# Loading the first eight chunks of q and k in pairs, eight rows a partition

## The chip, the cores and the metric

The kernel runs on one core of one Trainium2 chip. The metric is the device time of one execution in microseconds (us); the figure for the kernel before is the median of three runs. Engines are named as the profile names them: PE does matrix multiplies (PEld its weight loads), DVE vector work, ACT activations, POOL and SP here mostly issue DMAs. A DMA that changes the type of the data (float32 in memory, float16 on the chip) is called a casting load here, one that keeps float32 a direct load.

## The reference

Four batches of a cross-covariance attention, followed by one feed-forward block over all 24320 rows. N is 6080, C is 256, Dff is 2048, all inputs are float32 and tau is 1.

```python
qn = q / (norm(q, axis=1) + 1e-6)          # norms over the N rows, per column
kn = k / (norm(k, axis=1) + 1e-6)
s = kn.T @ qn / tau                        # 256 x 256 per batch
a = softmax(s, axis=-1)
x = (v @ a).reshape(4 * 6080, 256)
r = maximum(x @ w_in, 0)                   # 256 -> 2048
out = (s_moe * r * r + b) @ w_out          # 2048 -> 256
```

## The kernel before

**What is computed where.** For each batch, a 256 x 256 product of q and k over all 6080 rows (matmuls of line 154 into `s_ps`), the squared column norms of q and k, and from both a softmax matrix that is folded into `w_in` (`wa`). After that the batch needs only v: groups of 512 rows are transposed (`vT`) and multiplied with `wa` (line 761), squared, and multiplied with `w_out` (line 932, 836 and 808). Batches 1 to 3 have their q and k work spread over the steps of the v groups before them; only batch 0 has nothing to hide behind. It is the stage from 0 to about 38 us, and this change is made in it.

**Batch 0.** Its rows are cut into 13 chunks (`chunks_first`): eleven of 512 rows, four rows to a partition, then one of 256 and one of 192 rows. `load(c)` takes a tile `qk` (q and k of the chunk, 4 KB a partition) from the pool `qk_pool` of eight buffers and issues one DMA for k and one for q. Three of the first four transfers are direct loads into the float32 tile `raw32`: k of chunk 0 in two halves of 64 partitions, on the SP and the ACT queue, q of chunk 0 on the ACT queue, k of chunk 1 on the SP queue. `cast` then turns them into float16: the k parts on DVE, the q part on ACT (both are line 145 in the profile). All others are casting loads on the POOL queue (line 137), in order of chunk, k ahead of q. The last three chunks come with all three k parts first and then the q parts. Behind them in the same queue are v of the first group (line 458), `w_in` in five pieces (line 522), v, and `w_out` in four float32 pieces `w32` (line 537), which take buffers from the same pool and tag as `qk`.

**What a chunk does to the engines.** Eight matmuls of line 154; a square of k on ACT (line 185) and of q on DVE for even chunks (line 182) or on ACT for odd ones; two fold additions (line 199) and one addition into the running sum (line 213), all on DVE. Chunks 5 to 9 also have one or two idle matmuls (line 554), which only keep PE busy. After chunk 9 the squares of the late chunks 10 to 12 go to PE directly (lines 229, 179, 252), and then come a chain of logarithms and exponentials on ACT (line 277), the softmax (line 308) and the first block of `wa` (lines 329 to 359). The first matmul of line 761 follows.

**What sets the order.** Every instruction is kept in program order on its engine (`po`), and so are the DMAs of one queue. A load waits until all readers of the buffer's last contents are done: with eight buffers, chunk 8 takes the buffer of chunk 0, the `w_out` pieces those of four chunks of the middle, and in batch 1 chunks 4 to 7 those of the `w_out` pieces. The pieces are read until the casts of line 638 (`T3`), steps 34 to 40 of the main loop. Loads of later batches are put 16 steps ahead of their first matmul, but POOL runs ahead of that: it follows its own order, not the steps.

Of the kernel before, what the change touches and what calls it, by code (L numbers as in the profile page):

```python
# [8 lines left out]
FP16 = mybir.dt.float16  # L9
FP32 = mybir.dt.float32  # L10
# [6 lines left out]
def kernel(  # L17
# [12 lines left out]
    nc = tc.nc  # L30
    P = 128

    B, N, C = q.shape
# [17 lines left out]
    NLATE = 3  # L51
# [3 lines left out]
    def po(ins):  # L55

        tc.keep_in_program_order(ins)
        return ins

    def pool(name, bufs, **kw):  # L60
        return ctx.enter_context(tc.tile_pool(name=name, bufs=bufs, **kw))
# [1 line left out]
    PSUM = bass.MemoryType.PSUM  # L63
    consts = pool("consts", 1)
    wpool = pool("wpool", 1)
    qk_pool = pool("qk_pool", 8)
    sq_pool = pool("sq_pool", 2)
    late_pool = pool("late_pool", 1)
    f3_pool = pool("f3_pool", 13)
# [5 lines left out]
    gpool = pool("gpool", 2)  # L75
# [17 lines left out]


    JC = 4
    DIRECT = ((0, 0), (0, 1), (1, 0))
    NDIRECT = 2

    def make_chunks(rows_of):
        chunks, at = [], 0  # L100
# [11 lines left out]
    class Gram:  # L112


        def __init__(self, b, chunks):
            self.b, self.chunks = b, chunks
            self.tiles = {}
            self.raw, self.rows, self.n_ps = {}, ([], []), [None, None]

        def load(self, c, parts=(0, 1)):  # L120

            at, np_, jc = self.chunks[c]
            if 0 in parts:
                self.raw[c] = qk_pool.tile([P, 2, JC, C], FP16, tag="qk", name="qk")
            t = self.raw[c]
            for i in parts:
                src = (k, q)[i]
                rows = src[self.b, at : at + np_ * jc, :].rearrange("(p j) c -> p j c", j=jc)
                if self.b == 0 and (c, i) in DIRECT:
                    if c == i == 0:  # L130
                        for h, queue in enumerate((nc.sync, nc.scalar)):
                            ps = ts(h, P // 2)
                            queue.dma_start(out=raw32[ps, 0], in_=rows[ps])
                    else:
                        (nc.sync, nc.scalar)[i].dma_start(out=raw32[:, DIRECT.index((c, i))], in_=rows)
                else:
                    po(nc.gpsimd.dma_start(out=t[:np_, i, :jc, :], in_=rows))
            self.tiles[c] = t[:, 1], t[:, 0]

        def cast(self, c):  # L140

            qc, kc = self.tiles[c]
            for i, (dst, copy) in enumerate(((kc, nc.vector.tensor_copy), (qc, nc.scalar.copy))):
                if (c, i) in DIRECT:
                    po(copy(out=dst, in_=raw32[:, DIRECT.index((c, i))]))  # L145

        def start(self):
            self.s_ps = ps_gram.tile([P, CH, C], FP32, tag="s_ps", name="s_ps")
# [306 lines left out]
    def load_v(g):  # L455
        t0, nj = group(g)
        v16 = vpool.tile([P, TG // P, C], FP16, tag="v16", name="v16")
        po(nc.gpsimd.dma_start(  # L458
            out=v16[:, :nj, :],
            in_=v_flat[t0 : t0 + nj * P, :].rearrange("(p j) c -> p j c", j=nj)))  # L460
        v_tiles[g] = v16
# [30 lines left out]
    nc.vector.memset(ones32, 1.0)  # L492
    grams = {b: Gram(b, chunks_first if b == 0 else chunks_later) for b in range(B)}
    g0 = grams[0]
    raw32 = gpool.tile([P, len(DIRECT), JC, C], FP32, tag="g16", name="raw32")

    po(nc.scalar.preload_act_table_set("natural_log_exp_and_others"))
    tiny = consts.tile([P, 1], FP32)
# [2 lines left out]
    nc.vector.memset(eps, EPS)  # L501
    ones_id = consts.tile([P, P], FP16)
    po(nc.vector.tensor_copy(out=ones_id, in_=fill.bitcast(FP32)[:, :P]))
    for c in range(NDIRECT):
        g0.load(c)
        g0.cast(c)
    for c in range(NDIRECT, len(g0.chunks) - NLATE):
        g0.load(c)
        if c == NDIRECT:
            po(nc.gpsimd.affine_select(  # L510
                out=ident16, in_=ones_id, compare_op=ALU.is_equal, fill=0.0, base=0,
                pattern=[[-1, P]], channel_multiplier=1))

    for parts in ((0,), (1,)):
        for c in range(len(g0.chunks) - NLATE, len(g0.chunks)):
# [14 lines left out]
    w_out_rows = moe_w_out.rearrange("(fo p) d -> p fo d", p=P)  # L530
# [2 lines left out]
    NPIECE = FT // 4  # L533
    w_pieces = []
    for i in range(NPIECE):
        w32 = qk_pool.tile([P, 4, C], FP32, tag="qk", name="w32")
        po(nc.gpsimd.dma_start(out=w32, in_=w_out_rows[:, ts(i, 4), :]))
        w_pieces.append(w32)
    load_v(2)
    s_bc = consts.tile([P, 1], FP32)  # L540
    po(nc.gpsimd.dma_start(out=s_bc, in_=moe_s.to_broadcast((P, 1))))
# [126 lines left out]
    for i, f in enumerate(folds):  # L668
        early.setdefault(FOLDS[i], []).append(f)
    at_step(14, lambda: po(nc.vector.tensor_scalar_mul(  # L670
        out=s_out, in0=s_bc, scalar1=1.0 / (LAM * LAM))))
# [29 lines left out]
    for b in range(1, B):  # L701
# [6 lines left out]
        n = NCH * JC  # L708
# [247 lines left out]
    for s in range(NS + FT):  # L956
# [9 lines left out]
        if work:  # L966
            items, n = work[0]
# [61 lines left out]
```

## Time and profile before

| | |
|---|---|
| median of three runs | 714.37 us (714.33 to 714.67) |
| span of the profiled execution, first to last instruction | 712.9 us |
| what lies around the span, against the median | 1.5 us |
| PE busy | 692.9 us (97%) |
| DVE, ACT, POOL busy | 635.6, 547.5, 114.1 us |
| first matmul of batch 0 (line 154) | starts at 10.96 us |
| first matmul of the main loop (line 761) | starts at 37.84 us |
| mean clock granted to PE | 0.998 |

The span is what the profile sees, so every sum is made in it, and a difference in it is carried to the median unchanged. The profile has no total for its own execution apart from the span; the median lies 1.5 us above it. Of the views, the chain of waits says what ended last in each stretch; the timeline lists the instructions with the idle time of their engine ahead of them and what ended it; the table of windows gives busy times and the rate of the DMAs. That rate counts bytes as written to the destination: a casting load that reads 4 KB counts 2 KB, a direct one counts all it reads.

### The profile page before, as it was taken

To read this page: it belongs to the slowest core of one execution; us is meant where nothing else is said; L and a number is where in the kernel's file an instruction comes from. 1 tells how busy PE (TensorE), PEld (TensorE's weight loads), DVE (VectorE), ACT (ScalarE), POOL (GpSimd) and SP (SyncE) were. 2 spreads that over 40 slices of the span, in tenths; PEclk is the share of its full clock that TensorE was granted. 3 is DMA by queue.
4 is the path that set the end of the run, shared out by engine and by line. 5 is a ranking of instruction groups with operands and counts; after the bars stand their busy time and mean duration, and the time that the engine had idled before them with its cause. 6 is when DMAs were issued, how large, how long until landed. Compare 5 with 4: busy or idle time off the path is not lost.

```text
span 712.9 us, 17531 instructions
## 1 busy us (share of the span) xinstructions
PE 692.9 (97%) x7422; PEld 502.9 (71%) x7422; DVE 635.6 (89%) x906; ACT 547.5 (77%) x598; POOL 114.1 (16%) x192
## 2 busy tenths in 40 slices
PE   3699999999999999999999999999999999999998
PEld 2456777776677777777677777777768777777777
DVE  4889999999988989998999899998998888888886
ACT  5689877787777777778877777777876777777875
POOL 4533132201202222111010222111000000000000
PEclk9999999999999999999999999999999999999999
DMA  9999999566566878465761888737323333321202
GB/s 213 207 259 168 186 164 137 114 109 122 105 136 109 133 137 144 110 92 101 156 131 50 148 134 150 129 76 96 101 65 75 94 71 75 97 61 46 83 31 75
DMA packets 87854, 83.55 MB, mean 117 GB/s; under 512 B 56368, under 2 KB 62784, under 8 KB 87776
## 3 DMA queue, kind: packets, MB, share of 16 engines
q0 software_dynamic: 27136, 44.00, 38.9%
q1 hardware_dynamic: 60128, 37.45, 21.1%
q8 instruction: 58, 0.95, 0.6%
q10 hardware_dynamic: 512, 0.98, 0.4%
q14 instruction: 20, 0.16, 0.1%
HBM read 78.91 MB, written 24.90 MB: 146 GB/s over the span
## 4 chain that ended last, share of the span: by engine, by line
PE 95%; DMA 4%; ACT 1%; issue 0%; DVE 0%; ACTq 0%; POOLq 0%
PE h_ps L761 46%; PE o_ps L932 40%; PE s_ps L154 5%; DMA qk<-in_q_dram 2%; DMA qk<-in_k_dram 1%; PE wa_ps L394 1%; PE o_ps L836 1%; PE o_ps L808 0%; PE wa_ps L336 0%; ACT r L277 0%; PE n_ps L252 0%; ACT sq L185 0%; ACT eT L308 0%; PE vT_ps L469 0%; DVE half L229 0%
## 5 line engine op out<-in xcount | busy, mean ns | idle before, releaser
L771 ACT ACTIVATE r<-h_ps 128x1024 f16<-128x1024 f32 (+1 forms) x384 | 388.5, 1013 | 144.2 <-PE h_ps L761 140.6
L761 PE MATMUL h_ps<-vT,wa 128*128 128x512 f16 (+7 forms) x1632 | 452.1, 364 | 0.5 <-ACT wa L329 0.5
L932 PEld LDWEIGHTS <-S 128*128 128x128 f16 x2944 | 198.1, 98 | 84.3
L932 PEld LDWEIGHTS <-g 128*128 128x128 f16 x2208 | 155.0, 98 | 74.0
L784 DVE TENSOR_TENSOR g<-r 128x2048 f16<-128x2048 f16 (+2 forms) x150 | 174.4, 1163 | 10.1 <-ACT r L771 9.7
L932 PE MATMUL o_ps<-T,S 128*128 128x128 f16 x2208 | 183.1, 219 | 0.0
L761 PEld LDWEIGHTS <-wa 128*128 128x128 f16 x1632 | 136.6, 98 | 19.0 <-ACT wa L329 1.0
L932 PE MATMUL o_ps<-w_out,g 128*128 128x128 f16 x1472 | 134.2, 219 | 0.0
L782 ACT ACTIVATE g<-r 128x1024 f16<-128x1024 f16 (+1 forms) x97 | 100.3, 1034 | 0.2
L789 DVE SCALAR_TENSOR_TENSOR o_sb<-o_ps,s_out,u 128x256 f32<-128x256 f32 x138 | 66.2, 480 | 36.1 <-PE o_ps L932 34.5
L154 PE MATMUL s_ps<-qk 128*128 128x256 f16 (+1 forms) x384 | 71.0, 287 | 15.6 <-ACT qk L145 11.0
L458 POOL DMA_DIRECT2D v<-in_v_dram x48 | 31.4, 662 | 239.9 <-DMA vT<-v 192.7
L215 POOL DMA_DIRECT2D f<-f x33 | 28.8, 874 | 245.9 <-DVE f L199 197.3
L789 DVE SCALAR_TENSOR_TENSOR u<-o_ps,s_out,rowconst 128x256 f32<-128x256 f32 x138 | 65.7, 476 | 0.0
L932 PE MATMUL o_ps<-w_out,S 128*128 128x128 f16 x736 | 63.5, 219 | 0.0
L932 PE MATMUL o_ps<-N,g 128*128 128x128 f16 x736 | 63.4, 219 | 0.0
L185 ACT ACTIVATE sq<-qk 128x1024 f16<-128x1024 f16 (+2 forms) x53 | 54.5, 1041 | 4.5 <-DMA qk<-in_k_dram 1.9
L861 DVE TENSOR_TENSOR S<-S,g 128x2048 f16<-128x2048 f16 (+1 forms) x47 | 56.4, 1200 | 1.2
L859 DVE TENSOR_TENSOR S<-g 128x2048 f16<-128x2048 f16 (+1 forms) x47 | 56.0, 1192 | 0.0
L863 DVE TENSOR_TENSOR S<-g 128x2048 f16<-128x2048 f16 x46 | 55.8, 1214 | 0.0
L865 DVE TENSOR_TENSOR S<-g,S 128x2048 f16<-128x2048 f16 x46 | 55.8, 1213 | 0.0
L154 PEld LDWEIGHTS <-qk 128*128 128x128 f16 (+1 forms) x384 | 33.0, 103 | 21.2 <-ACT qk L145 11.0
(103 smaller groups left out, 334.4 us busy)
## 6 DMA issues: line engine op xcount, KB each, us to landing
out_dram<-o_sb SPq DMA_DIRECT2D x43, 512.0 KB, 3.0
v<-in_v_dram POOLq DMA_DIRECT2D x47, 256.0 KB, 5.0
qk<-in_q_dram POOLq DMA_DIRECT2D x43, 256.0 KB, 7.7
qk<-in_k_dram POOLq DMA_DIRECT2D x42, 256.0 KB, 6.4
f<-f POOLq DMA_DIRECT2D x30, 128.0 KB, 3.1
vT<-v SPq DMA_TRANSPOSE x182, 3.0
w<-in_moe_w_out_dram POOLq DMA_DIRECT2D x4, 512.0 KB, 9.9
out_dram<-o_sb SPq DMA_DIRECT2D x8, 256.0 KB, 4.1
```

The costliest lines, as they stand in the source:

```text
L154: po(nc.tensor.matmul(self.s_ps[:, ch, :], qc[:np_, j, ts(ch, P)], kc[:np_, j, :], start=(c == 0 and j == 0 and ch == 0), stop=(c == len(s ...
L185: po(nc.scalar.activation(out=st["sq"][:np_, a, js, :], in_=(qc, kc)[a][:np_, js, :], func=AF.Square))
L761: po(nc.tensor.matmul(dst, wa[:, ci, ts(m, P)], src, start=(ci == 0), stop=(ci == CH - 1), skip_group_check=True))
L771: po(nc.scalar.activation(out=r16[:, :, i % 2, :n], in_=h_tiles.pop((g, i))[:, :, :n], func=AF.Relu))
L782: po(nc.scalar.activation(out=dst, in_=src, func=AF.Square))
L784: po(nc.vector.tensor_mul(dst, src, src))
L789: po(nc.vector.scalar_tensor_tensor(out=dst, in0=src, scalar=s_out, op0=ALU.mult, in1=add, op1=ALU.add))
L859: po(nc.vector.tensor_add(T[1], A21, A22))
L861: po(nc.vector.tensor_sub(T[2], T[1], A11))
L863: po(nc.vector.tensor_sub(T[3], A11, A21))
L865: po(nc.vector.tensor_sub(T[4], A12, T[2]))
L932: po(nc.tensor.matmul(st[name][:, j, :], a()[:, i, ts(j, P)], w[:, i, :], start=first, stop=last, skip_group_check=True))
```

## The change

The first eight chunks of batch 0 are loaded as four pairs. One DMA brings k of both chunks of a pair and one DMA q, 512 KB read becoming 1 MB, and each partition reads eight rows (8 KB) that lie in one piece, where it read four rows (4 KB). The tile of a pair holds both chunks, so the pool has four buffers of 8 KB for eight of 4 KB. Single loads (batch 0 from chunk 8 on, and all of batches 1 to 3) fill one half of such a tile. Direct loads are now only k of the first pair, as two halves of 64 partitions on the SP and ACT queues; q of the first pair goes to the POOL queue with a cast. Both casts of `raw32` are on DVE, and the q cast on ACT is gone. The `w_out` pieces take two tiles of two pieces each. The `affine_select` that makes the identity stands behind the second pair's loads.

```diff
-    qk_pool = pool("qk_pool", 8)
+    qk_pool = pool("qk_pool", 4)
...
-    DIRECT = ((0, 0), (0, 1), (1, 0))
-    NDIRECT = 2
+    NPAIRS = 4
...
+        def place(self, c):
+
+            if c // 2 not in self.raw:
+                self.raw[c // 2] = qk_pool.tile([P, 2, 2 * JC, C], FP16, tag="qk", name="qk")
+            t = self.raw[c // 2][:, :, (c % 2) * JC : (c % 2 + 1) * JC]
+            self.tiles[c] = t[:, 1], t[:, 0]
+            return t
+
         def load(self, c, parts=(0, 1)):
 
             at, np_, jc = self.chunks[c]
-            if 0 in parts:
-                self.raw[c] = qk_pool.tile([P, 2, JC, C], FP16, tag="qk", name="qk")
-            t = self.raw[c]
+            t = self.place(c)
             for i in parts:
                 src = (k, q)[i]
                 rows = src[self.b, at : at + np_ * jc, :].rearrange("(p j) c -> p j c", j=jc)
-                if self.b == 0 and (c, i) in DIRECT:
-                    if c == i == 0:
-                        for h, queue in enumerate((nc.sync, nc.scalar)):
-                            ps = ts(h, P // 2)
-                            queue.dma_start(out=raw32[ps, 0], in_=rows[ps])
-                    else:
-                        (nc.sync, nc.scalar)[i].dma_start(out=raw32[:, DIRECT.index((c, i))], in_=rows)
+                po(nc.gpsimd.dma_start(out=t[:np_, i, :jc, :], in_=rows))
+
+        def load_pair(self, n):
+
+            for c in (2 * n, 2 * n + 1):
+                self.place(c)
+            at = self.chunks[2 * n][0]
+            for i in range(2):
+                rows = (k, q)[i][self.b, at : at + P * 2 * JC, :].rearrange("(p j) c -> p j c", j=2 * JC)
+                if n == 0 and i == 0:
+                    for h, queue in enumerate((nc.sync, nc.scalar)):
+                        ps = ts(h, P // 2)
+                        queue.dma_start(out=raw32[ps], in_=rows[ps])
                 else:
-                    po(nc.gpsimd.dma_start(out=t[:np_, i, :jc, :], in_=rows))
-            self.tiles[c] = t[:, 1], t[:, 0]
+                    po(nc.gpsimd.dma_start(out=self.raw[n][:, i], in_=rows))
 
         def cast(self, c):
 
-            qc, kc = self.tiles[c]
-            for i, (dst, copy) in enumerate(((kc, nc.vector.tensor_copy), (qc, nc.scalar.copy))):
-                if (c, i) in DIRECT:
-                    po(copy(out=dst, in_=raw32[:, DIRECT.index((c, i))]))
+            po(nc.vector.tensor_copy(out=self.tiles[c][1], in_=raw32[:, ts(c, JC)]))
...
-    raw32 = gpool.tile([P, len(DIRECT), JC, C], FP32, tag="g16", name="raw32")
+    raw32 = gpool.tile([P, 2 * JC, C], FP32, tag="g16", name="raw32")
...
-    for c in range(NDIRECT):
-        g0.load(c)
-        g0.cast(c)
-    for c in range(NDIRECT, len(g0.chunks) - NLATE):
-        g0.load(c)
-        if c == NDIRECT:
+    for n in range(NPAIRS):
+        g0.load_pair(n)
+        if n == 0:
+            for c in range(2):
+                g0.cast(c)
+        if n == 1:
             po(nc.gpsimd.affine_select(
                 out=ident16, in_=ones_id, compare_op=ALU.is_equal, fill=0.0, base=0,
                 pattern=[[-1, P]], channel_multiplier=1))
+    for c in range(2 * NPAIRS, len(g0.chunks) - NLATE):
+        g0.load(c)
...
     for i in range(NPIECE):
-        w32 = qk_pool.tile([P, 4, C], FP32, tag="qk", name="w32")
-        po(nc.gpsimd.dma_start(out=w32, in_=w_out_rows[:, ts(i, 4), :]))
-        w_pieces.append(w32)
+        if i % 2 == 0:
+            w32 = qk_pool.tile([P, 8, C], FP32, tag="qk", name="w32")
+        w_pieces.append(w32[:, ts(i % 2, 4)])
+        po(nc.gpsimd.dma_start(out=w_pieces[i], in_=w_out_rows[:, ts(i, 4), :]))
```

## The prediction

> **What bounds the kernel now.** I read the chain of waits first. From 37.84 us on nearly every piece of it is PE, which is busy for all but about 3 of the last 675 us; the change takes no matmul away there, so all it can do is move the start of that stretch. Ahead of it the chain is this (start, length, what):
>
> ```profile
> 1.30 7.22 DMA qk<-in_q_dram
> 8.80 10.44 DMA qk<-in_q_dram
> 19.28 1.05 PE s_ps L154 x8
> 21.00 9.47 DMA qk<-in_k_dram
> 30.49 1.06 ACT sq L185
> 32.06 0.95 PE n_ps L252 x7
> 33.03 0.48 ACT r L277
> ```
>
> Up to 30.49 us the path is loads of q and k; after that it is a short chain over ACT, DVE and PE. The timeline shows how regularly chunks arrive: PE starts chunks 5 to 9 at 19.28, 21.74, 24.30, 26.76 and 29.31 us, the first four after idling for the q load.
>
> ```profile
> 19.28 1.05 PE L154 MATMUL s_ps<-qk 128*128 128x256 f16 x8 [0.95 <-DMA qk<-in_q_dram]
> ...
> 26.76 1.66 PE L154 MATMUL s_ps<-qk 128*128 128x256 f16 x8 [1.18 <-DMA qk<-in_q_dram]
> ...
> 30.37 0.69 DVE L199 TENSOR_TENSOR f<-sq 128x1024 f16<-128x1024 f16 x1 [1.08 <-ACT sq L185]
> ```
>
> That is (29.31 - 19.28) / 4 = 2.51 us a chunk of 1.049 MB read, 418 KB/us. Ten chunks at this pace would begin at 29.31 - 25.1 = 4.2 us. The third view is the table of windows; its last two columns are the DMA share and the GB/s written:
>
> ```profile
> 2.00:4.00 2.00, 0.00 (x0) 0.00 (x0) 0.00 (x0) 0.09 (x1) 1.94 (x5) 1.00 0.86 211
> 4.00:6.00 2.00, 0.00 (x0) 0.00 (x0) 0.24 (x1) 0.00 (x0) 2.00 (x4) 1.00 1.05 257
> 6.00:8.00 2.00, 0.00 (x0) 0.00 (x0) 0.56 (x1) 0.00 (x0) 0.04 (x1) 1.00 1.05 339
> 8.00:10.00 2.00, 0.00 (x0) 0.00 (x0) 0.69 (x1) 0.14 (x1) 0.73 (x1) 1.00 1.11 267
> ...
> 18.00:20.00 2.00, 1.05 (x11) 0.70 (x9) 1.83 (x5) 1.65 (x2) 1.01 (x2) 1.00 1.11 207
> ```
>
> The DMA engines never rest between 4 and 30 us: they are the bound. But the first 10 us move less. Up to 10 us, 2 x (211 + 257 + 339 + 267) = 2148 KB were written; the three direct loads are 1573 KB of it, so 575 KB came from casts, which read 1150 KB. Together 2.72 MB were read from about 2.75 us, when the windows of 0.25 us first show steady traffic, in 7.25 us. At 418 to 420 KB/us this takes 6.5: some 0.77 us are lost while direct loads run.
>
> **Part 1: fewer direct bytes.** Direct loads fall from 1573 to 1049 KB; q of the first pair becomes a casting load. If the 0.77 us go with the direct bytes, a third goes: -0.26 us. A second row gives the same size. POOL's waits on the transfer eight back show the landings (start, issue time, idle ahead of it in brackets):
>
> ```profile
> 40.37 0.55 POOL L541 DMA_DIRECT2D s_bc<-in_moe_s_dram  x1 [0.58 <-DMA w_in<-in_moe_w_in_dram]
> 41.60 0.54 POOL L543 DMA_DIRECT2D b_bc<-in_moe_b_dram  x1 [0.68 <-DMA w_in<-in_moe_w_in_dram]
> 42.88 0.53 POOL L458 DMA_DIRECT2D v<-in_v_dram  x1 [0.74 <-DMA v<-in_v_dram]
> 44.66 0.53 POOL L458 DMA_DIRECT2D v<-in_v_dram  x1 [1.24 <-PE wa_ps L336]
> 46.15 0.53 POOL L137 DMA_DIRECT2D qk<-in_k_dram  x1 [0.96 <-DMA w<-in_moe_w_out_dram]
> 47.41 0.53 POOL L137 DMA_DIRECT2D qk<-in_q_dram  x1 [0.73 <-DMA w<-in_moe_w_out_dram]
> ```
>
> Casting loads of 524 KB (w_in, then v) land 1.23 and 1.28 us apart. The four uncast w_out pieces of 524 KB land about 1.49 us apart on average: by my count of the queue they free the issues from 44.66 to 49.15 us, 4.49 us for three gaps. One 524 KB load turned from direct to casting is then worth 1.25 - 1.49 = -0.24 us. I take -0.25; ends: 0 (the start-up loss has nothing to do with casts) and -0.77.
>
> **Part 2: 8 KB rows in the stream.** Seven casting loads of 1.049 MB replace thirteen of 0.524 MB. The trace has no 8 KB row. The w_in loads of the rows above read 2 KB pieces, the v load 4 KB pieces, and both take about 1.25 us for 524 KB: the length of a piece does not show. I take 0. Lower end: charge the whole difference of the 1 KB w_out pieces to the number of pieces (32 an engine against 8, 0.24 us, 0.01 us a piece); 8 KB rows save four pieces an engine per 524 KB, and fourteen such halves give -0.56 us. Upper end: the worst pace that the trace has for these rows, the 2.72 / 7.25 = 0.375 MB/us of the first stage, for all 7.34 MB: 7.34 x (1/0.375 - 1/0.418) = +2.0 us.
>
> Fewer loads do not mean fewer fixed costs on the path: up to eight are in flight and they land 1.25 us apart, back to back. The Trainium skill's "DMA: Bandwidth & Descriptors", section "Measured", puts a load at 2.0 us plus its bytes at 436 KB a us and asks for 1 MiB each. My estimate by that formula, with loads taken one after another, is 13 x 3.2 - 7 x 4.4, some 11 us gained, and 703.6 us in all; the landings above, 1.23 to 1.28 us apart, contradict it for a filled queue. Against the change speaks the same page's "SWDGE vs HWDGE vs iDMA", where a packet is preferably at most 4096 B; the page gives no price for a longer one, and this trace shows none, so it adds nothing to the sum.
>
> **Part 3: arrival in pairs.** With the stream's origin at 4.2 - 0.25, pair n is complete at 3.95 + 5.02 (n + 1): 8.97, 13.99, 19.01, 24.03 us; chunk 8 at 26.5, chunk 9 at 29.06 (29.31 before). The first k casts are on DVE, 0.80 and 0.69 us in the trace; ACT loses its q cast of 1.04 us, and PE can start near 9.1 for 10.96. None of that counts, as PE waits for loads from 19.28 us anyway. What may count is the last pair. DVE's cadence is 2.3 us for an even chunk (26.89 to 28.86, and 0.34 to the next start) and 1.53 for an odd one (25.36 to 26.89). From 24.03: chunk 6 to 26.3, chunk 7 to 27.9, chunk 8 to 30.2. The fold of chunk 9 needs ACT's square of its q, 1.06 after 29.06, so 30.12: it starts at 30.2, against 30.37 before. Of 0.25 us gained, about 0.07 are lost here: **+0.07**. Ends: 0, and +0.7 if the pair's second chunk (1.53 us of DVE) waits half its length longer than I count. PE has 16 matmuls for the pair, 2.1 us at full clock (1.05 for eight), 3.3 at the granted clock of 0.50 between 27 and 30.4 us (1.66 for eight), and is free again for chunk 8 or within a microsecond of it.
>
> **Part 4: fewer buffers.** The load of chunk 8 waits for all readers of chunks 0 and 1. ACT's three squares (about 1.0 each) and PE's 16 slow matmuls end near 12.4 us, the load was issued at 15.99 before. By then 8 MB are issued and 3.4 have arrived: 11 us of work lies in the queue. Likewise chunk 10 waits for chunks 2 and 3 (about 17.3, issued at 21.00) and chunk 12 for chunks 4 and 5 (about 22.3, issued at 23.59; 8 us of work queued). From there the limit of eight in flight rules as before. Without that cover each us of late issue past an empty queue would be a us on the path. The w_out pieces wait for chunks 6 to 9, free by 30.2; they are issued from 34.60. In batch 1, chunk 4 waits for two pieces: its load moves from 66.37 to 68.54, where chunk 5's was, behind the cast of line 638; queued behind it are chunk 5 and a v load, which move by about 1 us, and chunk 6 then waits for the last cast, ending at 71.63. Chunk 4 is first read at 83.02, and a load lands within 10 us. Cost 0. The `affine_select` (0.34 us) goes behind one more issue; its reader starts at 35.39. Cost 0.
>
> **Sum.** -0.25 + 0 + 0.07 = -0.18 us on the span of 712.9, and so on the median: 714.2 us. A measurement of this kernel can tell about 0.2% (1.4 us) from no change; this is well inside.
>
> **Rivals.**
> *The stream gains more.* The direct loss goes whole (-0.77) and pieces have a price (-0.56): at most -1.33, 713.0; the middle is 713.5. For it: the first windows write unevenly. Against: w_in and v rows cost the same per byte, and DVE is nearly full from 24 us. Chance 0.18, of which 0.05 passes 0.2%.
> *8 KB rows are slower.* A longer piece holds an engine longer, and three queues share it at the start. Each per cent on 7.34 MB (17.6 us) costs 0.18 us; with the 0.18 gained, from 9% on the kernel is slower by 0.2%. At the pace of the first stage, 716.2 us. For it: direct and cast together ran at that pace. Against: 2 KB and 4 KB rows are equal. Chance 0.15, of which 0.12 passes 0.2%.
> *The bunches bind.* DVE or PE comes late out of pairs 2 and 3, and the start-up gain turns into +0.3 to +0.8: about 714.9. The granted clock is part of it: it fell to 0.50 at 27.0 us after 3.4 us of part-idle PE, and if such a spell falls on 33 to 37 us, where some 1.5 us of matmuls are on the chain, it adds up to 1.5. Chance 0.14, of which 0.02 passes 0.2%.
> *The rows are moved in 4 KB pieces anyway.* Then part 2 is exactly 0 and the time is the forecast's, 714.2; the packet count tells. It has 0.1 of the forecast's chance of 0.53.
>
> The likeliest case spans 713.9 to 714.6. The range takes in most of the other cases: 713.3 to 715.4. Faster by over 0.2%: 0.05; slower: 0.14; within: 0.81.
>
> **What would show it.** Packets should fall by 1024 from 87854. The first line 154 matmul should start near 9.1 us, chunk 9 near 29.05, the fold at about 30.2 and line 761 near 37.65. Chunk 9 spaced more than 2.55 us from chunk 8, or chunks 8 and 9 later than 26.8 and 29.3, would make part 2 wrong; DVE busy without a gap past 30.4 would make part 3 wrong; a rest in DMA share before 30 us part 4.

## The result, and the profile after

| | before | changed |
|---|---|---|
| median of 7 runs each | 714.45 us (714.33 to 715.45) | 716.44 us (715.80 to 716.97) |
| span of the profiled execution | 712.9 us | 715.0 us (own time 716.69) |
| first matmul of batch 0 | 10.96 us | 10.34 us |
| first matmul of the main loop | 37.84 us | 38.69 us |
| PE waits for q in batch 1 | none | 0.76 us, at 84.79 us |
| DMA packets | 87854 | 86702 |

The changed kernel takes 1.0026 times as long, with an interval of 1.0015 to 1.0036. It is slower by 2.0 us, where 0.2 us faster was forecast. Every execution with both figures spends 1.7 to 1.8 us around its span, so before's profiled one took some 714.6, and the two profiles differ by 2.1 us, the medians by 2.0.

In the changed kernel line 154 has become 161, line 761 is 771, line 137 is 134 for single loads and 148 for pairs, line 199 is 206 and line 638 is 648. The timeline shows PE's first matmuls of each pair, then those of chunks 7, 8 and 9 (start, length, in brackets the idle time ahead):

```profile
10.34 3.59 PE L161 MATMUL s_ps<-qk 128*128 128x256 f16 x16 [10.34 <-DMA qk<-in_q_dram]
15.22 1.92 PE L161 MATMUL s_ps<-qk 128*128 128x256 f16 x16 [1.28 <-DMA qk<-in_q_dram]
20.18 2.65 PE L161 MATMUL s_ps<-qk 128*128 128x256 f16 x16 [3.04 <-DMA qk<-in_q_dram]
25.05 1.89 PE L161 MATMUL s_ps<-qk 128*128 128x256 f16 x8 [1.80 <-DMA qk<-in_q_dram]
...
30.07 1.05 PE L161 MATMUL s_ps<-qk 128*128 128x256 f16 x8
...
84.79 0.39 PE L161 MATMUL s_ps<-qk 128*128 128x256 f16 x2 [0.76 <-DMA qk<-in_q_dram]
```

The pairs follow each other every 4.88, 4.96 and 4.87 us, a little faster than the 5.02 forecast. It is the first pair that is late: 10.34 for 8.97. So the loss lies ahead of 10.3 us. The windows of that stretch (the last two columns are the DMA share and the GB/s written) show DMA engines nearly as busy as before, with less written:

```profile
4.00:6.00 2.00, 0.00 (x0) 0.00 (x0) 0.00 (x0) 0.00 (x0) 1.51 (x3) 1.00 1.05 229
6.00:8.00 2.00, 0.00 (x0) 0.00 (x0) 0.00 (x0) 0.00 (x0) 0.00 (x0) 1.00 0.94 188
8.00:10.00 2.00, 0.00 (x0) 0.00 (x0) 1.30 (x2) 0.85 (x1) 0.00 (x0) 1.00 1.10 221
```

Which queue takes the time is seen in the view of the DMA queues for 2 to 10 us. Its columns are packets, MB written, and the time of the packets as a share of the 16 engines. First the kernel before, then the changed one:

```profile
q0 software_dynamic: 312, 0.58, 38.2%
q1 hardware_dynamic: 224, 0.79, 32.2%
q10 hardware_dynamic: 224, 0.79, 31.3%
```

```profile
q0 software_dynamic: 184, 0.69, 42.8%
q10 hardware_dynamic: 80, 0.52, 30.5%
q1 hardware_dynamic: 80, 0.52, 29.2%
```

Queues q1 and q10 carry the direct loads; q0 carries the casting ones. With the casting bytes counted as they are read, twice those written, the changed kernel has read 2.4 MB by 10 us, before 2.7. A half of 64 rows has 80 packets, of which 16 are small ones; I leave such packets out of the counts. The share times 8 us times 16 engines is engine time: before 63.5% of 128 = 81.3 us for 384 direct rows of 4 KB, **0.212 us a row**; changed 59.7% of 128 = 76.4 us for 128 rows of 8 KB, **0.597 us a row**. The direct bytes fell by a third and their engine time by 6%. Of the 184 casting packets 16 are small, so the 168 casting rows of 8 KB took 54.8 / 168 = 0.326 us each. (The expectations below have 0.298 and 0.30 for it, which counts the small packets as rows.)

### The profile page after: what moved, and what is told of

Its sections match the earlier page's. It is cut to its first block, busy times and chain, and to the rows that moved or that the text cites. A ratio compares the mean times of both kernels' runs of the same rounds, so it can differ in the third digit from the quotient of the medians.

```text
span 715.0 us, 17494 instructions
## 1 busy us (share of the span) xinstructions
PE 692.4 (97%) x7422; PEld 502.3 (70%) x7422; DVE 635.7 (89%) x906; ACT 547.0 (77%) x597; POOL 110.8 (16%) x186
## 2 busy tenths in 40 slices
DMA packets 86702, 83.29 MB, mean 116 GB/s; under 512 B 56240, under 2 KB 62656, under 8 KB 86496
## 4 chain that ended last, share of the span: by engine, by line
PE 92%; DMA 6%; ACT 1%; issue 0%; POOL 0%; DVE 0%; POOLq 0%; ACTq 0%
PE h_ps L771 45%; PE o_ps L942 39%; PE s_ps L161 4%; DMA qk<-in_k_dram 4%; DMA qk<-in_q_dram 2%; PE wa_ps L401 1%; PE o_ps L846 1%; PE o_ps L818 0%; PE wa_ps L343 0%; ACT r L284 0%; POOL qk L148 0%; PE n_ps L259 0%; ACT r L781 0%; ACT sq L192 0%; ACT g L792 0%
```

## The experiments

The first set asks where the first pair loses its time, and whether the wait in batch 1 comes from the late issue there. All times below are medians of their own set, beside a median of before of 714.39 to 714.50 us; "main loop" is the start of its first matmul.

**The halves, with 4 KB rows** (changed kernel):

```diff
-                    for h, queue in enumerate((nc.sync, nc.scalar)):
-                        ps = ts(h, P // 2)
-                        queue.dma_start(out=raw32[ps], in_=rows[ps])
+                    for js in (slice(0, JC), slice(JC, 2 * JC)):
+                        for h, queue in enumerate((nc.sync, nc.scalar)):
+                            ps = ts(h, P // 2)
+                            queue.dma_start(out=raw32[ps, js], in_=rows[ps, js])
```

> Against the changed kernel (first pair's q landed at 10.32 us, chunk 9 at 30.06, main loop from 38.69, 716.44 us). The two 64-partition halves stay, but each is loaded in two DMAs of 4 KB rows. Theory 'halves' (a direct load of 64 partitions costs an engine twice the time per byte, whatever its row length: 0.597 us per 8 KB row in the changed kernel where a casting row of 8 KB takes 0.298): direct rows take about 0.30 us per 4 KB, first pair still at 10.2 to 10.5, chunk 9 at 29.9 to 30.2, 716.4. Rival 'long rows' (8 KB direct rows are slow, 4 KB rows are not): 0.15 to 0.21 us per 4 KB row, first pair at about 9.0, chunk 9 at about 28.8, main loop from 37.5, 715.2.

Measured: 714.83 us, ratio 1.0004 (0.9994 to 1.0013), main loop 37.88, first pair 9.74.

**One DMA of 128 partitions, 8 KB rows** (changed kernel):

```diff
-                    for h, queue in enumerate((nc.sync, nc.scalar)):
-                        ps = ts(h, P // 2)
-                        queue.dma_start(out=raw32[ps], in_=rows[ps])
+                    nc.sync.dma_start(out=raw32, in_=rows)
```

> k of the first pair in one DMA of 128 partitions on the SP queue, rows of 8 KB kept. Theory 'halves': 0.30 us per direct 8 KB row instead of 0.597; 128 x 0.29 / 16 = 2.3 us of engine time come back, first pair at about 8.0 to 8.6 us, chunk 9 at about 27.8 to 28.4, main loop from 36.5 to 37.1, 714.3 to 714.9. Rival 'long rows': still about 0.6 us a row, first pair at 10.2 to 10.5, 716.4.

Measured: 713.73 us, ratio 0.9989 (0.9980 to 0.9999), main loop 36.51, pairs at 8.18, 13.10, 18.01 and 22.93.

**Two DMAs of 128 partitions, split along the row** (changed kernel):

```diff
-                        ps = ts(h, P // 2)
-                        queue.dma_start(out=raw32[ps], in_=rows[ps])
+                        js = ts(h, JC)
+                        queue.dma_start(out=raw32[:, js], in_=rows[:, js])
```

> k of the first pair in two DMAs of 128 partitions with 4 KB rows, chunk 0 on SP, chunk 1 on ACT. Both theories expect the direct rows at 0.15 to 0.21 us per 4 KB. 'Halves': first pair at 8.0 to 8.6 us, chunk 9 at 27.8 to 28.4, main loop from 36.5 to 37.1, 714.3 to 714.9, as with one DMA of 8 KB rows. 'Long rows': gains as well, while the one DMA of 8 KB rows does not.

Measured: 713.72 us, ratio 0.9988 (0.9978 to 0.9997), main loop 36.67, pairs at 8.24, 13.28, 18.16 and 23.12. The queue views of the three, in their order, are taken from 0 to 12 us here, as eight rows of a load of 128 partitions start ahead of 2 us:

```profile
q0 software_dynamic: 349, 1.30, 54.6%
q1 hardware_dynamic: 160, 0.52, 13.5%
q10 hardware_dynamic: 160, 0.52, 13.2%
```

```profile
q0 software_dynamic: 400, 1.51, 62.5%
q1 hardware_dynamic: 144, 1.05, 24.9%
```

```profile
q0 software_dynamic: 396, 1.49, 62.4%
q1 hardware_dynamic: 144, 0.52, 14.1%
q10 hardware_dynamic: 144, 0.52, 10.7%
```

All three move the same 1.05 MB of k. Their engine time is 26.7%, 24.9% and 24.8% of 12 x 16 = 192 us, so 51.3, 47.8 and 47.6 us, against 76.4 us in the changed kernel (39.8% in the same window):

| direct load of k of the first pair | us a row | us per 4 KB |
|---|---|---|
| two halves of 64 partitions, 8 KB rows (the change) | 0.597 | 0.299 |
| four of 64 partitions, 4 KB rows | 0.200 | 0.200 |
| one of 128 partitions, 8 KB rows | 0.373 | 0.187 |
| two of 128 partitions, 4 KB rows | 0.186 | 0.186 |

So neither the length of a row nor the split of the partitions is the cause alone. 8 KB rows are no dearer per byte in a load of 128 partitions; halves cost 8% more at 4 KB, and 60% more at 8 KB. The means take in the first rows, which are slow in every version: the eight that start ahead of 2 us in the one DMA took 0.96 us each. From 3 to 5 us, behind them, the views of the changed kernel and of the one DMA say:

```profile
DMA packets 72, 0.48 MB, mean 242 GB/s; under 512 B 13, under 2 KB 13, under 8 KB 13
DMA packets 108, 0.84 MB, mean 418 GB/s; under 512 B 4, under 2 KB 4, under 8 KB 8
```

Nearly all of it is direct, and the DMA share is 1.04 and 1.01: 0.57 us a row of 8 KB in the halves, 0.31 in the whole load. With 4 KB rows the halves' extra cost is over by 5 us: from 5 to 10 us, with casting loads beside them, their rows took 0.172. Those halves also lose what no row shows: from 3 to 4 us the DMA share is 0.69, where the one DMA has 1.03. Taking the halves away brings 2.0 to 2.2 us at the main loop, and the kernel is then faster than before by 0.7 us.

**The casts of the `w_out` pieces earlier** (changed kernel). Cast steps 34, 36, 38, 40 free the buffers in batch 1; here the first two are done together:

```diff
-    CT3 = (34, 36, 38, 40)
+    CT3 = (34, 34, 38, 40)
```

> The changed kernel with the T3 cast of the second w_out piece moved from step 36 to step 34, beside that of the first. Theory 'buffer of two pieces' (batch 1's chunk 4 waits for both pieces, its load is issued 2.2 us later and lands after PE wants it): chunk 4 is issued near 67.5 us instead of 69.38, the 0.76 us wait of line 161 near 84 us goes, 715.5. Rival 'crowded DMA engines' (the transposes of 66 to 72 us hold the load up whenever it is issued in that stretch): the load is issued earlier but lands at 84 to 85 all the same, the wait stays, 716.4. The first stage is not touched: main loop from 38.7 by both.

Measured: 715.73 us (715.49 to 715.81), ratio 1.0015 (1.0006 to 1.0024), main loop 38.73. Chunk 4 of batch 1 is issued at 67.56 instead of 69.38, and PE doesn't wait. The chain of the changed kernel shows what that load does there (start, length):

```profile
69.38 0.52 POOL qk L134
69.90 14.84 DMA qk<-in_q_dram
```

Its windows from 72 us, and then those with the casts moved:

```profile
72.00:74.00 2.00, 2.00 (x24) 1.52 (x22) 2.00 (x4) 2.00 (x4) 1.10 (x3) 1.00 2.03 212
74.00:76.00 2.00, 2.00 (x22) 1.42 (x21) 2.00 (x4) 1.37 (x2) 0.00 (x0) 1.00 1.00 34
76.00:78.00 2.00, 2.00 (x23) 1.48 (x22) 2.00 (x4) 1.77 (x2) 0.00 (x0) 1.00 1.37 52
```

```profile
72.00:74.00 2.00, 2.00 (x24) 1.48 (x23) 2.00 (x4) 2.00 (x4) 1.06 (x2) 1.00 1.17 254
74.00:76.00 2.00, 2.00 (x22) 1.45 (x21) 2.00 (x4) 1.41 (x2) 0.00 (x0) 1.00 1.08 174
76.00:78.00 2.00, 2.00 (x24) 1.44 (x22) 2.00 (x4) 1.73 (x2) 0.00 (x0) 1.00 1.14 202
```

The first of them is a spell in which the DMA engines are busy and write almost nothing: 34 and 52 GB/s for 174 and 202. The load of 14.84 us spans it.

The second set tests both findings from the side of before, and asks more closely about the rows.

**Before, casts swapped** (`CT3 = (36, 34, 40, 38)`):

> The kernel before, with the T3 casts of line 638 exchanged in pairs, so that batch 1's chunk 4 waits for a cast of step 36, not 34, and chunk 6 for one of step 40. Nothing else is changed; the first stage keeps its 37.84 us. Theory 'late release in batch 1': chunk 4 is issued at 68.0 to 68.6 us for 66.37, its successors land later, and somewhere between 80 and 130 us PE waits for a q load of line 154: 0.3 to 0.9 us, 714.7 to 715.3. Rival 'that wait needs the pair loads': chunk 4 is issued as late, PE has no such wait, 714.4.

Measured: 714.45 us, ratio 1.0001 (0.9992 to 1.0011). Chunk 4 was still issued at 66.26, as the buffers are single there and the load, it seems, took the one that came free first. The edit delayed nothing, so this run says nothing on its question.

**Before, k of chunk 0 in one DMA:**

```diff
-                        for h, queue in enumerate((nc.sync, nc.scalar)):
-                            ps = ts(h, P // 2)
-                            queue.dma_start(out=raw32[ps, 0], in_=rows[ps])
+                        nc.sync.dma_start(out=raw32[:, 0], in_=rows)
```

> The kernel before, with k of chunk 0 as one direct load of 128 partitions on the SP queue instead of two halves on two queues. Theory 'halves': the mean direct row of 4 KB falls from 0.212 us to about 0.17, (0.212 - 0.17) x 384 / 16 = 1.0 us of engine time, so chunk 5's matmuls start near 18.3 (19.28 before) and the main loop near 36.9 (37.84), 713.4. Rival 'only long rows in halves cost': the halves here have 4 KB rows, so at most 0.2 us come back, 714.2.

Measured: 714.29 us, ratio 0.9999 (0.9990 to 1.0008), main loop 37.38 (37.84 in before). The direct rows took 52.9% of 128 us for 384, 0.176 a row for 0.212. The saved 0.036 x 384 / 16 = 0.86 us an engine bring 0.46 us; the total doesn't tell it from nothing.

**The casting rows cut to 4 KB** (k of the first pair split along the row as above):

```diff
-                    po(nc.gpsimd.dma_start(out=self.raw[n][:, i], in_=rows))
+                    for js in (slice(0, JC), slice(JC, 2 * JC)):
+                        po(nc.gpsimd.dma_start(out=self.raw[n][:, i, js], in_=rows[:, js]))
```

> The kernel with k of the first pair in two DMAs of 128 partitions (pairs complete at 8.24, 13.28, 18.16, 23.12 us, main loop from 36.67, 713.72 us), with each casting load of a pair now cut into two DMAs of 4 KB rows; the buffers and the arrival in pairs stay. Theory 'longer casting rows stream faster': pairs 5.02 us apart for 4.96, pair 3 at 23.3 to 23.5, main loop from 36.9 to 37.0, 714.0. Rival 'the row length of a casting load does not show': pair 3 at 23.0 to 23.2, 713.7.

Measured: 715.03 us, ratio 1.0008 (0.9998 to 1.0017), main loop 38.39, 1.72 us later than with whole rows. The loss is made by the second pair, complete at about 14.8 us for 13.28; from chunk 4 (18.53) to chunk 6 (23.53) the pace is 5.0 us a pair, no worse than before's. Its 4 KB pieces lie 8 KB apart in memory, which those of before don't, so the 1.72 us are not the price of row length alone. Its casting rows that start from 5 to 7 us took about 0.25 us, those from 8 to 10 us 0.176; that makes some 0.6 us an engine. Why those rows are slow, and where the rest is lost, stays open.

**Both halves on one queue** (changed kernel):

```diff
-                    for h, queue in enumerate((nc.sync, nc.scalar)):
+                    for h, queue in enumerate((nc.sync, nc.sync)):
```

> The changed kernel with both 64-partition halves of the first k (8 KB rows) on the SP queue, one behind the other. Theory 'a half is slow by itself' (64 partitions, whatever runs beside it): rows still take 0.5 to 0.6 us, first pair at 10.0 to 10.5, main loop from 38.4 to 38.8, 716.2. Rival 'two halves at once are slow' (the two queues' halves get in each other's way): rows near 0.31 us, first pair at 8.2 to 8.8, main loop from 36.6 to 37.2, 714.0 to 714.6.

Measured: 716.13 us (715.07 to 716.89), ratio 1.0024 (1.0014 to 1.0033), main loop 38.17.

```profile
q1 hardware_dynamic: 160, 1.05, 52.6%
q0 software_dynamic: 197, 0.74, 48.7%
```

52.6% of 128 us for 128 rows is 0.526 us a row. Two halves at once on two queues are about a third of the price over 0.373; the rest is still there on one queue.

The third set looks for a better version and for the limits of both causes.

**Before, all casts late** (`CT3 = (37, 37, 40, 40)`):

> The kernel before with the T3 casts of line 638 at steps 37, 37, 40, 40 for 34, 36, 38, 40: now no w_out piece is free before step 37, so batch 1's chunk 4 is issued near 69.3 us (66.37 before) and chunk 5 right behind it, as with the buffers of two pieces. Theory 'late release': loads of batch 1 crowd with the transposes and PE waits for a q load somewhere between 80 and 130 us in some executions: 714.6 to 715.3 and a spread of the runs of about 1 us. Rival 'that wait needs the pair buffers': no wait, 714.4, spread as before.

Measured: 714.33 us, ratio 1.0001 (0.9992 to 1.0010). Chunk 4 is issued at 70.13, later than in the changed kernel, and PE doesn't wait. A late issue alone doesn't bring the wait.

**The one DMA and the split rows, with `CT3 = (34, 34, 38, 40)`:**

> Both causes taken away from the changed kernel: k of the first pair as one DMA of 128 partitions with 8 KB rows, and the second piece's T3 cast at step 34. The first stage as with the one DMA alone (main loop from 36.5, 1.33 us earlier than before), the wait near 113 us (0.35) gone: 714.4 - 1.3 = 713.1. Rival: the wait stays or comes elsewhere, 713.7 as with the one DMA alone.

> The same with k of the first pair in two DMAs of 128 partitions and 4 KB rows on two queues: main loop from 36.7, 713.2 (714.4 - 1.17); 713.7 if the casts do nothing.

Measured: 713.68 us, ratio 0.9988 (0.9979 to 0.9997), main loop 36.57; and 713.66 us, ratio 0.9989 (0.9980 to 0.9997), main loop 36.48. Neither waits in batch 1. These are the fastest versions, 0.75 us (0.1%) below before, and with 713.72 without the moved casts hardly faster than the split alone. The main loop begins 1.3 us earlier, so half of the gain is not in the total. In the two profiles all of it is still there at the last DVE instruction (708.73 and 708.64 us for 710.00); from its start to the end of the span they take 3.31 and 3.05 us, before 2.86. That stretch is 2.85 to 3.56 us in the kernels with pairs, 2.85 to 2.94 in those with single buffers. I found no cause for that.

**The halves as casting loads** (changed kernel, no `raw32` and no casts of it):

```diff
-                        queue.dma_start(out=raw32[ps], in_=rows[ps])
+                        po(nc.gpsimd.dma_start(out=self.raw[0][ps, 0], in_=rows[ps]))
```

> The changed kernel with k of the first pair as two casting loads of 64 partitions on the POOL queue, ahead of q, without the float32 tile and the two casts on DVE. Theory 'a half of 64 partitions is slow whatever its type': its 8 KB rows take 0.5 to 0.6 us for 0.30, 128 x 0.27 / 16 = 2 us lost, first pair at 9.7 to 10.5 us, main loop from 38.2 to 38.8, 716. Rival 'only float32 written into a half is slow': rows of 0.30 us, first pair at 7.8 to 8.6, main loop from 36.4 to 37.0, 713.7 to 714.5.

Measured: 717.24 us (five runs, 716.24 to 718.97), ratio 1.0038 (1.0024 to 1.0052). The first pair starts at 9.34, at the edge of what the first theory expects, but not for its reason. The halves come first in the queue: 34 of their 128 rows start ahead of 4 us and took 0.70 us each, like the slow first rows elsewhere. The view from 4 to 6 us has the rest of them:

```profile
q0 software_dynamic: 123, 0.41, 102.2%
```

Without 24 small packets that is 99 rows at 102.2% of 32 us, 0.33 us each, as casting rows of 128 partitions take (0.326). So once under way halves are not dear on the casting path. What is late is the start: the casting k moves its first row only after 2.6 us, where the one direct DMA has eight rows under way by 2 us. The main loop is late for another reason (38.97): PE waits 1.14 us, until 35.69, for the last square of q; why it comes late there is open.

The last set is about the wait in batch 1, which the changed kernel has in some executions.

**Before, with an issue at the changed kernel's moment** (`CT3 = (36, 36, 38, 40)`):

> The kernel before with the T3 casts at steps 36, 36, 38, 40. Batch 1's chunk 4 should be issued 30.6 to 31.2 us after the start of the main loop, as in the changed kernel (30.7), where casts at 37 had put it at 32.4 and the kernel before at 28.5. Theory 'moment': loads issued at that moment, between the transposes of 28 to 33 us after the main loop's start, run into a spell of some 5 us in which the DMA engines move under 100 GB/s, in a part of the executions; then runs above 714.9 in more than 2 of 10, and a spell between 72 and 90 us if the profile meets one. Rival 'the pair buffers or pair loads are needed': runs as tight as before (714.1 to 714.7, at most one outlier), 714.4.

**The changed kernel, casts still later** (`CT3 = (37, 37, 40, 40)`):

> The changed kernel with the T3 casts at 37, 37, 40, 40: chunk 4 issued still later, near 71 us, 32.4 us after the main loop's start. Theory 'moment': no or fewer spells, no wait of line 161, runs within 0.5 us of 715.8. Rival 'the later the worse': the wait near 84 us grows from 0.8 to 2 to 2.5 us, 717.5 to 718.

**The changed kernel, as it is:**

> The changed kernel once more, unchanged, for its spread: main loop from 38.6 to 38.8 us in any execution; runs in two groups, near 715.8 without a wait in batch 1 and 716.4 to 717.0 with one, each with at least a third of the runs. If the wait is fixed and not met by chance, all runs lie within 0.5 us and the profile shows 0.7 to 0.9 us of wait near 84 us.

Measured: 714.44 us, ratio 1.0000 (0.9991 to 1.0009); 715.72 us (715.41 to 715.96), ratio 1.0015 (1.0006 to 1.0024); 715.93 us (715.58 to 716.64, and one of 720.03), ratio 1.0026 (1.0015 to 1.0036). The issues of chunk 4, in this order; ahead of them the changed kernel's first profile:

```profile
69.38 0.53 POOL L134 DMA_DIRECT2D qk<-in_k_dram  x1 [5.52 <-ACT T L648]
```

```profile
68.27 0.54 POOL L137 DMA_DIRECT2D qk<-in_k_dram  x1 [5.55 <-ACT T L638]
```

```profile
71.33 0.53 POOL L134 DMA_DIRECT2D qk<-in_k_dram  x1 [7.21 <-ACT T L648]
```

Measured from the start of the main loop, the first and the second are at the same moment (30.7 and 30.6 us after it), and the kernel before doesn't wait. The third is 2 us later than the changed kernel's own, and doesn't wait either. In the third kernel of the set, chunk 4 is issued at 69.29, and its profile has no wait; it has a milder spell (101 and 132 GB/s from 74 to 78 us). Its executions do spread. Of the 18 of the changed kernel in two sets, 10 lie between 715.58 and 715.98 and 8 at 716.19 or above. The 21 with the casts moved, earlier or later, all lie between 715.41 and 715.96. So the wait belongs to the changed kernel with its own cast steps, in part of its executions, as far as their times tell; only one profile shows it. Two more kernels with pairs and these steps have a shorter one, later: 0.62 us at 115.56 in the halves with 4 KB rows, 0.35 at 113.73 in the one DMA. It isn't the lateness of the issue as such. What sets off the spell of the DMA engines stays open.

## Why the prediction was wrong

**The stage, part 1: the step that failed.** "One 524 KB load turned from direct to casting" was priced at 1.25 - 1.49 = -0.25 us. The added casting load cost about what was counted: 64 rows of 0.326 us on 16 engines, 1.30 us. The removed direct time was mis-sized: it fell not by 1.49 but by (81.3 - 76.4) / 16 = 0.31 us. The balance is +0.99 instead of -0.25, which is 1.24 of the 1.37 us by which the first pair is late; the pairs behind it give 0.35 back, and the main loop begins 0.85 us later than before's. I counted direct loads by their bytes, from `w_out` pieces that use 128 partitions and short rows, and did not see what became of the remaining ones: before, a third of the direct bytes came in halves of 64 partitions with 4 KB rows, and now all of them do, with 8 KB rows. The runs settle this: undone, the first pair starts at 8.2 and the main loop at 36.5 to 36.7.

The 0.77 us that before loses in its first 10 us I laid on direct loads as such. The one-DMA version of before shows that 0.46 of it were its halves.

Engine time is not path time everywhere: four halves with 4 KB rows save 1.6 us of it per engine against the change (25.1 / 16) and bring 0.81 at the main loop, as before's one DMA brings half of what it saves. With one DMA in the changed kernel it is (76.4 - 47.8) / 16 = 1.79 us saved and 2.18 brought; part of the difference is that its rows start ahead of 2 us, where the halves move nothing before 2.17.

The Trainium skill bears on this in "SBUF — State Buffer", section "Can I just issue two DMAs to hit both halves?": two DMAs at once, one to each half, reached only 6% more than a single one of them there, and only a transfer of all 128 partitions reaches all ports. The 242 GB/s of the two halves against 418 of the whole load agree in sign. The page does not speak of the length of a row, on which the price depended here (8% at 4 KB, 60% at 8 KB), nor of casting loads, whose halves were not dear once under way, so these runs don't show that the ports are the whole cause.

**Part 2: right, slightly mis-sized.** Casting rows of 8 KB were taken as 0. The pairs come 4.90 us apart on average for 5.02, three times 0.12 = -0.35 us, inside the bounds; chunk 9 is 1.01 us late where the first pair was 1.37. The packets fell by 1152: the 1024 rows of the forecast, and 16 small ones for each of eight loads fewer. So the rows were not cut up. The formula of 2.0 us and 436 KB a us that the prediction quotes stands in the Trainium skill's "DMA: Bandwidth & Descriptors", section "Anatomy of one DMA — SWDGE (gpsimd) path"; the section "Measured" asks for the 1 MiB.

**Part 3: right.** As forecast, DVE comes out of the last pair without a gap (it is not idle from 25.03 to 31.19 us) and starts the fold of chunk 9 0.09 us after ACT's square for it ends at 31.10; 0.07 was forecast as the cost. So the sign "DVE busy without a gap past 30.4" appeared, though it cost no more than that:

```profile
31.19 0.68 DVE L206 TENSOR_TENSOR f<-sq 128x1024 f16<-128x1024 f16 x1
```

It is 0.99 us later than forecast because the last pair is 1.02 late. The granted clock was 0.50 from 22 to 28 us, while PE waited for loads; chunk 9's eight matmuls took 1.05 us again.

**Part 4: right in batch 0, failed in batch 1.** POOL waits 8.96 us to issue chunk 8, until 14.47, and the DMA share is 1.02 or more in every 2 us from 10 to 30: the DMA engines never rest. But "a load lands within 10 us" did not hold in batch 1: 14.84 us, and 0.76 us of PE. In the profile, what PE and DVE do runs 0.84 us behind before up to 80 us and 1.78 behind it from 94 us to the last DVE instruction (711.78 for 710.00).

**The sum as it was:** +0.85 (stage) + 0.94 (wait and what follows, this execution) + 0.3 (end) = 2.1 us. Stage and end alone come to 1.15; the kernels with the casts moved, which don't wait, are 1.2 to 1.3 us above before in their sets (715.72 and 715.73).

**The rivals.** "8 KB rows are slower" had the right sign, and 716.2 us near the measured time, by the wrong mechanism: it put the price on all 7.34 MB, and the casting rows grew no dearer. "The bunches bind" came to 0.09 us, far from its 0.3 to 0.8. "The stream gains more" did not happen; only without the halves does the main loop begin 1.2 to 1.3 us earlier than before's, near that rival's most of 1.33.

## What to carry to other kernels

When a change makes some DMAs fewer, look at the shape of those that stay: how many partitions each spans and how long a row is, and take a price only from rows of the same shape. A direct load of 128 partitions, if it is split between queues at all, is better split along the row than between partitions. When buffers become fewer and larger, the next stage that takes from the pool is where to look for a wait, and a single profile may or may not show it.

## What was not expected of the hardware

- A row of 8 KB in a direct load of 64 partitions took 0.597 us of an engine, in one of 128 partitions 0.373; with 4 KB rows 0.200 and 0.186. On one queue the halves still took 0.526. As casting loads their rows took 0.33 once under way, no more than those of whole loads. From 3 to 5 us the direct halves wrote 242 GB/s, the one DMA 418.
- Casting rows of 8 KB came 2% faster than 4 KB ones (4.90 us for 2.1 MB read, for 5.02), and cutting them in two at a stride of 8 KB cost 1.7 us of the stage.
- From 74 to 78 us, in batch 1, the DMA engines of the changed kernel showed a share of 1.00 and 1.37 and wrote 34 and 52 GB/s; with the casts moved it was 1.08 and 1.14, and 174 and 202 GB/s.
